# Cosine attention and a hard-swish layer: the fourth query tiles of a pair's two heads on two column halves of TensorE

## The chip, the cores and the metric

The kernel runs on one core of a Trainium2 chip. The metric is the device time of one execution in microseconds; a kernel's figure is the median of several executions. Profiles and traces come from one profiled execution.

## The reference

Attention over 8 batches and 12 heads, sequence length 448, head dimension 64. Queries and keys are divided by their norms, scores are divided by tau and go through a softmax; the result, laid out as 3584 tokens of 768 features, goes through a feed-forward layer with a hard-swish.

```
q_n = q / (norm(q) + 1e-06);  k_n = k / (norm(k) + 1e-06)
attn = softmax(q_n @ k_n^T / tau)
x = (attn @ v) as [3584, 768]
h = x @ w_in                       # 768 -> 2048
out = (h * clip(h + 3, 0, 6) / 6) @ w_out   # 2048 -> 768
```

## The kernel before

**Tiling.** Two heads are worked on together as a pair; there are 48 pairs, six for each batch. The 448 tokens are cut into three tiles of 128 and a rest of 64. Scores are computed transposed: keys on the 128 partitions, queries along the free dimension. The keys of a pair fall into four groups (`GROUPS`, L364): in groups 0 to 2 each head has a 128-key tile of its own (A0 and B0, A1 and B1, A2 and B2), and group 3, "M", joins the last 64 keys of both heads in one 128-partition tile. `scores` (L367) makes a group's scores in PSUM: for groups 0 to 2 two matmuls on the two 64-row halves of the array, since the head dimension is 64; for group 3 one matmul with all 128 rows, against `km`, which holds both heads' keys block by block. `exps` (L400) writes the exponentials as bf16 to an `at` tile, [128 keys, 1 or 2 heads, 512 queries]; its columns 448 to 511 are padding that was set to 1 once (L680).

**Value products.** `values(i, g)` (L421) multiplies one group's exponentials with the values. `at` is the stationary operand, 128 queries at a time, so that the result has queries on partitions. The moving operand is `vx`: 64 value columns and a column of ones for each head, 65 columns, so that the sum of the softmax comes out beside the result. There are four query tiles j; the fourth holds 64 queries and 64 columns of padding. In groups 0 to 2 each head has four matmuls of 65 columns (eight in a group); in group M each query tile has one matmul of 130 columns, as both heads' values lie side by side with zeros where the other head's keys are. All 28 matmuls of a pair add up in one PSUM tile `PV`, [128, 2 banks, 512]; `pv_out(j)` (L414) gives the place of query tile j in it, [128, 2 heads, 65]: tiles 0 and 1 in the first bank, 2 and 3 in the second. The first product in each bank starts the accumulation for the whole bank.

**After the products.** `finish_values(i)` (L444) runs on VectorE: the reciprocal of the eight sums (L453), then one multiplication of all of `PV` with them into the bf16 tile `on` (L454). A transposing DMA on SP's queue (`back_crossbar`, L485, for one pair, `back_two`, L497, for two) brings `on` to `xT`, where tokens are along the free dimension. When a batch's six pairs are there, `mm1_unit` (L513) does a 128-wide slice of the first feed-forward matmul, with the hard-swish on ScalarE (L522) and VectorE (L528), and `mm2_unit` (L549) a slice of the second, with copies out (L560, L562) and stores (L570).

**Order.** The order of every engine's queue is written out by hand. Up to pair 17 a list of strings, `PLAN`, gives it; from pair 18 a loop (L699) does. An iteration i of the loop issues the scores of pair i, groups 0 to 2, with their exponentials; the value products of pair i - 1, groups 1 to 3; `finish_values(i - 1)`; the scores of pair i, group 3; then the transposing DMA, the feed-forward units that belong to this iteration, the preparation of later pairs (squares, norms, transposes, loads); and last the value products of pair i, group 0.

```
for g in range(1, 4):
    if ("VA", i - 1, g) not in issued:
        do("VA", i - 1, g)
do("FI", i - 1)
do("SC", i, 3)
do("EX", i, 3)
```

So TensorE sees, in each iteration: six score matmuls on 64-row halves, 20 value products, one score matmul with all rows, a few dozen feed-forward matmuls, and 8 value products. After the last pair its remaining products follow directly, then the feed-forward units that are left.

Of the kernel before, what the change touches and what calls it, by code (L numbers as in the profile page):

```python
# [11 lines left out]
ALU = mybir.AluOpType  # L12
# [3 lines left out]


FIRST = 18
ORDER = "111111111111111111111111111111222222"

PLAN = [
# [40 lines left out]
def kernel(  # L62
# [10 lines left out]
    nc = tc.nc  # L73
    B, H, S, D = q.shape
# [8 lines left out]
    SM = 384  # L83
# [60 lines left out]
    def needs(*what):  # L144
        for w in what:
            assert w in issued or any(x < 0 for x in w[1:] if isinstance(x, int)), w
# [217 lines left out]
    GROUPS = [("A0", "B0"), ("A1", "B1"), ("A2", "B2"), ("M",)]  # L364
# [49 lines left out]
    def pv_out(j):  # L414
        return PV[:, j // 2, 0:260].rearrange("p (j h e) -> p j h e", j=2, h=2)[:, j % 2, :, :]


    def q_cols(b, j):
        return slice(128 * j, 128 * j + 128)

    def values(i, g):  # L421
        needs(("VC", i), ("FI", i - 1), *([("VA", i, g - 1)] if g else []))
        at = at_of.pop((i, g))
        vt = vx[i % NVX]
        last = g == len(GROUPS) - 1
        for n, name in enumerate(GROUPS[g]):
            for j in range(4):
                if name == "M":
                    o, mv = pv_out(j), vt[:, 3:5, :]
                else:  # L430
                    h = "AB".index(name[0])
                    o, mv = pv_out(j)[:, h, :], vt[:, 5 * h + int(name[1]), :]
                nc.tensor.matmul(  # L433
                    o,
                    at[:, n, q_cols(i // HP, j)],
                    mv,
                    start=(name == "A0" and j % 2 == 0),
                    stop=last,
                    skip_group_check=True,
                )  # L440

    twin_on = {}

    def finish_values(i):  # L444
        needs(*(("VA", i, g) for g in range(4)))
        if i % 2 == 0:
            needs(("BK", i - 4), ("BK", i - 3))
            twin_on[i // 2] = sb.tile([128, 2, 4, 2, D], BF16, name="on", tag="on", bufs=2)
        rc = sb.tile([128, 2, 4], FP32, name="rc", tag="rc", bufs=2)
        on = twin_on[i // 2][:, i % 2, :, :, :]  # L450
        on_of[i] = on
        pv4 = PV[:, :, 0:260].rearrange("p b (n e) -> p b n e", e=D + 1)
        nc.vector.reciprocal(out=rc[:, :, :], in_=pv4[:, :, :, D])  # L453
        nc.vector.tensor_tensor(  # L454
            out=on[:, :, :, :].rearrange("p (b j) h d -> p b (j h) d", b=2),
            in0=pv4[:, :, :, 0:D],
            in1=rc[:, :, :].to_broadcast([128, 2, 4, D]),
            op=ALU.mult,
        )

    def back(i, bank=None):
        z, key = bank_of(bank, 1)
        if bank is not None:
            z = z[:, :].bitcast(BF16)
        z_of[-1 - i] = z, key
        on = on_of.pop(i)
        for j in range(4):
            c, e = (slice(128 * j, 128 * j + 128), slice(0, 128)) if j < 3 else (slice(SM, S), slice(0, SR))
            if bank is not None:
                c = slice(128 * j, 128 * j + 128)  # L470
                nc.tensor.transpose(z[:, c], on[:, j, :, :], ident[:, :])
                continue
            nc.tensor.matmul(z[:, c], on[:, j, :, :], ident[:, e], start=True, stop=True)
# [164 lines left out]
    def whole_units(n):  # L638
# [7 lines left out]
        "LQ": load_qk, "LV": load_v, "W": next_weights, "SQ": square, "RE": reduce, "NO": norms,  # L646
        "NM": normalise, "VC": vcast, "TR": transposes, "XD": crossbar, "XB": back_crossbar, "XP": back_two, "CQ": copy_q, "CK": copy_k, "CS": copy_k3, "SC": scores,
        "EX": exps, "VA": values, "FI": finish_values, "BK": back, "CX": copy_x, "U": unit, "UA": lambda: finish_units("a"), "UV": lambda: finish_units("v"),
        "UU": whole_units, "D": busy, "DP": busy_pv, "OPEN": open_ring,
    }  # L650

    def do(op, *args):
        OPS[op](*args)
        key = (op,) + tuple(a for a in args if isinstance(a, int))
        if op not in ("RE", "NM", "LQ"):
            issued.add(key[:3] if op == "SC" else key)
# [31 lines left out]
    by_kind = {"1": [u for u in stream if u[0] is mm1_unit], "2": [u for u in stream if u[0] is mm2_unit]}  # L688
    first = [by_kind[x].pop(0) for x in ORDER]
    stream = first + [u for u in stream if u not in first]  # L690
# [5 lines left out]

    if FIRST + 6 < NP:
        do("LQ", FIRST + 6)
    for i in range(FIRST, NP):  # L699
        n_u = len(units[i])  # L700
# [84 lines left out]
```

## Time and profile before

| | |
|---|---|
| median of 8 runs | 424.08 us (422.91 to 426.73) |
| the profiled execution | 424.15 us, of which the trace's span is 422.4 us |
| value products (L433) | 1152 of 65 columns, 192 of 130 columns |
| their weight loads | 1344 of 128 columns, 98 ns each, overlapping the matmuls |
| feed-forward matmuls (L513) | 768 of 448 columns |
| feed-forward matmuls (L549) | 880 of 384 columns, 32 of 192 |
| `on` (L454) | 48 of 691 ns |

The duration of a matmul in the trace is modelled[...]: a 65-column product is shown with 194 ns, but the next one starts about 30 ns later. What a matmul costs on a full queue is therefore read from the distance between starts, not from its duration. `128*128` or `64*64` in a line is the part of the array (rows by columns) that the instruction uses.

### The profile page before, as it was taken

The numbers are of one execution on the slowest core, as the hardware profiler recorded it, in microseconds if no ns is written. First come the engines' busy times: TensorE is split into PE (matmuls) and PEld (weight loads), VectorE is DVE, ScalarE is ACT, GpSimd is POOL, SyncE is SP. The second block draws the span as 40 slices with busy tenths as digits, with TensorE's granted clock in tenths as the row PEclk, the third lists the DMA queues.
The fourth block names the chain that finished last, engine by engine and source line by source line (L and its number), as shares of the span: only waits on it lengthen the run. The fifth ranks groups of instructions, "written<-read, shape, count | busy, mean of one in ns | idle before, by whom it ended". The sixth has DMA issues, their size and how long they took to land.

```text
span 422.4 us, 9241 instructions
## 1 busy us (share of the span) xinstructions
PE 412.4 (98%) x3591; PEld 244.2 (58%) x3591; DVE 218.0 (52%) x420; ACT 271.3 (64%) x588; POOL 179.9 (43%) x187
## 2 busy tenths in 40 slices
PE   7999999999999999999999999999999999999996
PEld 5656465555656556555556555555655555655564
DVE  6778778756435544465445554555554343315410
ACT  4999888887648656757756775776765775105400
POOL 7697783363047256266365465364462200000000
PEclk9999999999999999999999999999999999999999
DMA  8999999997775867966974858757864431330033
GB/s 305 266 244 163 245 253 214 258 215 206 175 173 116 183 179 137 188 167 131 193 187 120 199 146 171 173 160 147 188 151 80 84 67 33 70 75 21 0 76 75
DMA packets 93740, 65.82 MB, mean 156 GB/s; under 512 B 58240, under 2 KB 92160, under 8 KB 93696
## 3 DMA queue, kind: packets, MB, share of 16 engines
q1 hardware_dynamic: 89904, 58.89, 60.9%
q0 software_dynamic: 3712, 6.29, 8.1%
q8 instruction: 28, 0.46, 0.5%
q14 instruction: 16, 0.13, 0.2%
q10 hardware_dynamic: 80, 0.05, 0.1%
HBM read 47.19 MB, written 11.01 MB: 138 GB/s over the span
## 4 chain that ended last, share of the span: by engine, by line
PE 90%; DMA 5%; DVE 1%; POOL 1%; issue 1%; ACT 1%; SPq 0%; POOLq 0%; ACTq 0%
PE M L549 23%; PE M L513 22%; PE PV L433 11%; PE Z L513 7%; PE Y L549 6%; PE M L394 6%; PE Y L513 5%; PE Z L549 5%; DMA raw<-in_k_dram 4%; PE Z L394 1%; PE PV L620 1%; DMA xT<-on 1%; PE Y L394 1%; PE SC L394 1%; DVE n L215 1%
## 5 line engine op out<-in xcount | busy, mean ns | idle before, releaser
L549 PEld LDWEIGHTS <-gT 128*128 128x128 bf16 x912 | 88.7, 98 | 58.4
L412 ACT ACTIVATE at<-M 128x448 bf16<-128x448 f32 x200 | 97.1, 566 | 31.1 <-PE M L394 28.7
L513 PEld LDWEIGHTS <-w_in_sb 128*128 128x128 bf16 x768 | 73.6, 98 | 66.1 <-issue 3.0
L513 PE MATMUL M<-xT,w_in_sb 128*128 128x448 bf16 x510 | 104.7, 353 | 0.1
L549 PE MATMUL M<-w_out_sb,gT 128*128 128x384 bf16 x592 | 100.8, 326 | 0.0
L246 POOL TENSOR_TENSOR nrm<-raw,r 128x896 bf16<-128x896 f32 (+1 forms) x46 | 75.3, 1639 | 33.4 <-ACT r L234 23.0
L528 DVE SCALAR_TENSOR_TENSOR gT<-u,M 128x448 bf16<-128x448 bf16 x85 | 52.4, 620 | 51.1 <-ACT u L522 49.7
L203 POOL TENSOR_TENSOR sq<-raw 128x896 f32<-128x896 f32 (+2 forms) x39 | 63.7, 1632 | 11.4 <-DMA raw<-in_q_dram 6.8
L433 PEld LDWEIGHTS <-at 128*128 128x128 bf16 x1344 | 53.7, 98 | 23.2 <-issue 15.9
L522 ACT ACTIVATE u<-M,bias 128x448 bf16<-128x448 f32 x85 | 54.9, 649 | 17.7 <-PE M L513 16.4
L433 PE MATMUL PV<-vx,at 128*128 128x65 bf16 (+1 forms) x1344 | 63.6, 198 | 0.0
L351 POOL COPY km<-tT 64x128 bf16<-64x128 bf16 x34 | 9.8, 289 | 107.4 <-DMA tT<-nrm 52.4
L215 DVE TENSOR_REDUCE n<-sq 128x14 f32<-128x896 f32 (+1 forms) x50 | 51.5, 1040 | 3.1 <-POOL sq L203 2.6
L560 ACT COPY o<-M 128x384 f32<-128x384 f32 x18 | 8.7, 481 | 41.2 <-PE M L549 39.3
L562 DVE COPY o<-M 128x384 f32<-128x384 f32 x19 | 10.6, 558 | 47.0 <-PE M L549 34.2
L454 DVE TENSOR_TENSOR on<-PV,rc 128x512 bf16<-128x512 f32 x48 | 33.2, 691 | 1.7
L394 PE MATMUL M<-tT,kz 64*128 64x448 bf16 (+1 forms) x178 | 33.4, 354 | 0.3 <-ACT at L412 0.3
L412 ACT ACTIVATE at<-Y 128x448 bf16<-128x448 f32 x47 | 26.6, 566 | 9.7 <-PE Z L394 9.7
L549 PE MATMUL Y<-w_out_sb,gT 128*128 128x384 bf16 (+1 forms) x192 | 31.9, 319 | 0.0
L513 PE MATMUL Z<-xT,w_in_sb 128*128 128x448 bf16 x144 | 31.2, 353 | 0.0
L412 ACT ACTIVATE at<-Z 128x448 bf16<-128x448 f32 x47 | 26.6, 566 | 7.1 <-PE M L394 4.1
L265 POOL CAST vx<-vr 128x512 bf16<-128x512 f32 x43 | 26.1, 612 | 5.7 <-DMA vr<-in_v_dram 5.1
(73 smaller groups left out, 329.7 us busy)
## 6 DMA issues: line engine op xcount, KB each, us to landing
vr<-in_v_dram SPq DMA_DIRECT2D x96, 128.0 KB, 4.2
raw<-in_q_dram SPq DMA_DIRECT2D x24, 448.0 KB, 4.5
raw<-in_k_dram SPq DMA_DIRECT2D x24, 448.0 KB, 4.5
out_dram<-o SPq DMA_DIRECT2D x110, 96.0 KB, 2.2
w_in_sb<-in_moe_w_in_dram POOLq DMA_DIRECT2D x4, 768.0 KB, 13.9
w_out_sb<-in_moe_w_out_dram POOLq DMA_DIRECT2D x4, 768.0 KB, 10.8
tT<-nrm SPq DMA_TRANSPOSE x34, 3.1
xT<-on SPq DMA_TRANSPOSE x29, 4.0
```

The costliest lines, as they stand in the source:

```text
L203: engines[e].tensor_tensor(out=o, in0=i, in1=i, op=ALU.mult)
L215: nc.vector.tensor_reduce(out=n2s[d % 2][:, j % 2, c], in_=sq[:, :, :, :].rearrange("p g c d -> p (g c) d")[:, c, :], axis=AX.X, op=ALU.add,)
L246: engines[e].tensor_tensor(out=nrm[:, :, g, :].rearrange("p c g d -> p g c d"), in0=raw_of[j][:, g, :, :], in1=rs[d % 2][3][:, j % 2, :] . ...
L265: (engines[e].copy if e == "a" else engines[e].tensor_copy)(out=o, in_=f)
L394: nc.tensor.matmul(o, ks, qt[rows], start=True, stop=True)
L412: nc.scalar.activation(out=o, in_=x, func=AF.Exp, scale=inv_tau)
L433: nc.tensor.matmul(o, at[:, n, q_cols(i // HP, j)], mv, start=(name == "A0" and j % 2 == 0), stop=last, skip_group_check=True,)
L454: nc.vector.tensor_tensor(out=on[:, :, :, :].rearrange("p (b j) h d -> p b (j h) d", b=2), in0=pv4[:, :, :, 0:D], in1=rc[:, :, :].to_broad ...
L513: nc.tensor.matmul(ps[:, 0:S], w_in_sb[:, cc, fc * 128 : (fc + 1) * 128], x[:, cc, 0:S], start=(cc == 0), stop=(cc == CC - 1),)
L522: nc.scalar.activation(out=u[:, :], in_=ps[:, 0:S], func=AF.Relu, bias=half_bias, scale=1.0 / 6.0)
L528: nc.vector.scalar_tensor_tensor(out=g[:, fc, c0 : c0 + S], in0=u[:, :], scalar=1.0, in1=ps[:, 0:S], op0=ALU.min, op1=ALU.mult,)
L549: nc.tensor.matmul(ps[:, 0:width], lhs, w_out_sb[:, fc, cols], start=(fc == 0), stop=(fc == FCN - 1),)
```

## The change

From pair 19 on (`TAILS`), the fourth query tile is left out of the products of each group. Its 64 queries are done behind the group M products of the same pair: for each of the four groups and each of the two heads one matmul with 64 columns of `at` (without the padding) as the stationary operand and 65 moving columns. Head 0's results go to partitions 0 to 63 of the fourth tile's place in `PV`, head 1's to partitions 64 to 127, so that the two heads' matmuls use the left and the right 64 columns of the array. For group M the 64 rows of the other head are cancelled by the zeros in `vx`, as before. Since head 1's queries of the fourth tile now lie on partitions 64 to 127, `finish_values` gets a third VectorE instruction, which multiplies that block with its reciprocals and writes it to partitions 0 to 63 of `on`, where the large multiplication had put something else.

```diff
+TAILS = 19
...
         last = g == len(GROUPS) - 1
+        tail = i >= TAILS
         for n, name in enumerate(GROUPS[g]):
-            for j in range(4):
+            for j in range(3 if tail else 4):
...
                     start=(name == "A0" and j % 2 == 0),
-                    stop=last,
+                    stop=last and not tail,
                     skip_group_check=True,
                 )
-
+        if not tail:
+            return
+        tail_of.append((g, at))
+        if not last:
+            return
+        for g, at in tail_of:
+            for h in range(2):
+                m = len(GROUPS[g]) == 1
+                nc.tensor.matmul(
+                    pv_out(3)[64 * h : 64 * h + 64, h, :],
+                    at[:, 0 if m else h, SM:S],
+                    vt[:, 3 + h if m else 5 * h + g, :],
+                    start=False,
+                    stop=m,
+                    skip_group_check=True,
+                )
+        tail_of.clear()
+
+    tail_of = []
...
             op=ALU.mult,
         )
+        if i >= TAILS:
+            nc.vector.tensor_tensor(
+                out=on[0:64, 3, 1, :],
+                in0=pv4[64:128, 1, 3, 0:D],
+                in1=rc[64:128, 1, 3:4].to_broadcast([64, D]),
+                op=ALU.mult,
+            )
```

## The prediction

> **What bounds the kernel now.** I read the page first: busy shares, then the slices with the granted clock.
>
> ```profile
> span 422.4 us, 9241 instructions
> PE 412.4 (98%) x3591; PEld 244.2 (58%) x3591; DVE 218.0 (52%) x420; ACT 271.3 (64%) x588; POOL 179.9 (43%) x187
> PE   7999999999999999999999999999999999999996
> PEclk9999999999999999999999999999999999999999
> ```
>
> TensorE is at 98%, VectorE at 52%, and the clock is whole. A busy PE can hide bubbles, because matmul ends are modelled, so I asked for the stretch that the change touches (pairs 19 to 47; their products run from 134 to 361 us) and then for the chain of waits inside one pair, number 35.
>
> ```profile
> core 0: us, PE busy (x) PEld busy (x) DVE busy (x) ACT busy (x) POOL busy (x), PEclk, DMA share, GB/s
> 161.00:361.00 200.00, 199.93 (x1735) 117.53 (x1734) 97.07 (x173) 131.33 (x295) 88.67 (x87) 1.00 0.64 142
> ```
>
> ```profile
> 261.33 2.60 PE Y L549 x16
> 263.94 0.24 PE PV L433 x8
> ...
> 264.85 0.08 PE Y L394
> 264.93 0.83 PE PV L433 x20
> 265.76 0.19 PE Z L394
> 265.95 0.19 PE M L513
> ```
>
> The chain never leaves PE in this pair. Over the 200 us one wait stands on it, 0.24 us at 176.7 us. So in this stretch a nanosecond more or less on TensorE's own queue is a nanosecond on the end.
>
> The same lines price a value product. Eight 65-column ones take 0.24 us, 0.030 each; over all 1056 neighbours in the instruction records the step from start to start is 30.9 ns in the mean (29 median), and 58 ns for the 130-column ones. In the x20 line 16 x 0.031 + 4 x 0.058 = 0.73 of 0.83 us; the other 0.10 us is something else. It stands where the score matmuls, which use 64 rows of the array (`64*128`), give way to full ones (`128*128`). I looked for such places where no semaphore can be the reason.
>
> ```profile
> 19.17 0.40 PE L433 MATMUL PV<-vx,at 128*128 128x130 bf16 x4
> 19.50 0.38 PE L391 MATMUL SC<-tT,kz 64*64 64x448 bf16 x2
> 19.81 0.28 PE L291 MATMUL Z<-ident,nrm 128*128 128x128 bf16 x2
> ```
>
> ```profile
> 63.95 0.39 PE L291 MATMUL Z<-ident,nrm 128*128 128x128 bf16 x4
> 64.26 0.36 PE L394 MATMUL M<-tT,kz 64*128 64x448 bf16 x2
> 64.56 0.55 PE L513 MATMUL M<-xT,w_in_sb 128*128 128x448 bf16 x2
> ```
>
> Read the starts (first column). The last of the four 130-column products starts at 19.17 + 0.40 - 0.22 (its modelled length) = 19.35 and streams for 0.058, to 19.41; the `64*64` pair starts at 19.50: 94 ns of nothing (151 - 57 in the records). Both its members start 3 ns apart and stream 448 columns in 0.187 to 0.189 us (six of L513 take 1.13 in the chain), to 19.69; the next full matmul starts at 19.81: 118 ns. At 64 us it is 98 in and 105 out. At 264.0 us, into the scores of the pair above, it is 96, and 39 neighbours of that kind in the trace have nearly the same step (median 125, mean 125.8 ns from start to start, 29 of it streaming). So each change of array shape costs about 95 ns in and 94 to 119 ns out, every time, and no other work lies beside it.
>
> **What the skill says.** "TensorEngine Tiling (Array Packing)", Key Properties: a change of tiling mode, as against a change of tile within a mode, drains TensorE. The gaps above agree, and in size they repeat. Its Restrictions add that column tiling turns fast weight load off. The trace has no `128*64` matmul; the nearest loads, 64 columns wide, are these:
>
> ```profile
> L433 PEld LDWEIGHTS <-at 128*128 128x128 bf16 x1344 | 53.7, 98 | 23.2 <-issue 15.9
> L391 PEld LDWEIGHTS <-kz 64*64 64x64 bf16 x12 | 0.6, 103 | 0.6 <-issue 0.2
> ```
>
> Half the columns, yet 103 against 98 ns, which fits. "TensorE: Matmul & The Clock Gate", Part 3, The mechanism, says that tiles of one mode start about 4 ns apart and run side by side; the trace shows 3 to 4 ns for row halves, nothing for column halves. The same page, LDWEIGHTS, prices a load by columns / 1.2 ns without the fast form: 53 ns for 64, used below as an estimate.
>
> **The change, part by part.** In the built program exactly TensorE's and VectorE's lists differ; ACT, POOL and SP have the same instructions in the same order with the same kinds of waits.
>
> Removed, for each of 29 pairs: query tile 3 of six 65-column groups and of the joint group, each with its load. 6 x 30.9 + 58 = 243 ns.
>
> Added on TensorE: eight loads and eight 65-column matmuls on `128*64` tiles, alternating between column 0 and column 64, between the joint group's third product and the pair's last score matmul (L394 on km, full shape). Both neighbours are full shape, so the block costs two changes of shape of its own; neither falls together with the change that the scores already pay, which lies 20 products earlier.
>
> - In: 94 ns (the `64*64` case). Out: 118 ns. The 3 ns of the second half, and 10 ns on the step behind (the second full matmul after a change starts 39 ns after the first at 264.9 us instead of 29). Together 225 ns. From the other side, by the row-halves' cheapest figures, 96 + 94 = 190.
> - Streaming: if halves run side by side and the loads go ahead behind the running matmul, four steps of 30.9 = 124 ns. If the halves go one by one, or the two loads of a step do, eight such steps, 247 ns. If a 53 ns load also stands in front of each step, 4 x (53 + 29) = 328.
>
> I take 225 + 124 = 349. The `64*64` gaps favour the two loads of a step going in parallel: its way out is 14 ns longer than the row halves' (302 against 288 ns from the last matmul's start to the next load), about the stream of 32 more columns, counted once and not twice. Net 349 - 243 = +106 ns a pair, x 29 = +3.1 us.
>
> Added on VectorE: one 64x64 multiply out of PSUM behind each pair's large one, waiting for it on VectorE itself (L454, 0.69 us). Nearest row:
>
> ```profile
> L313 DVE COPY kz<-Y 64x64 bf16<-64x64 bf16 x8 | 1.5, 187 | 0.5 <-PE Y L291 0.4
> ```
>
> With some 30 ns for the wait (the reciprocal, 208 ns, is followed 241 ns after its start) 0.22 us, 29 times, 6.4 us of VectorE work. Queued behind it are the products of hardswish (gT), which are not ready then (idle 1.49 us before the next one), and the transfer of `on` to xT, which SP issues later anyway:
>
> ```profile
> 266.04 0.69 DVE L454 TENSOR_TENSOR on<-PV,rc 128x512 bf16<-128x512 f32 x1
> ...
> 269.11 1.24 SPq L485 DMA_TRANSPOSE xT<-on  x1
> ```
>
> `on` is done at 266.73, SP comes to the transfer at 269.11 behind four V loads: 2.4 us of cover. For pair 47 the transfer does follow at once (362.37), but its reader, the first product with that batch's xT, is at 379.07, 12 us after landing. PV's next writer starts some 4 us later. I cost it at nothing; without cover it would be at most 0.2 us in each of five batches, 1 us. The `at` and V buffers stay read a little longer, to the end of the same pair; their next writers come a whole pair later, and no wait is added for them. The last score matmul, and its exponential, come 0.1 us later; ACT is at 66% in this stretch (131.33 of 200).
>
> Sum: +3.1 us on the profiled execution, 424.15 us with a span of 422.4 and 1.75 around it; that is 0.07 above the median of 424.08. From the median: **427.1 us**, +0.7%.
>
> **Rivals.**
>
> - A, the forecast: two drains, halves side by side, loads hidden. +60 to +150 ns a pair, 425.8 to 428.5. For: every change of shape in the trace drains, and row halves do run together. 52%.
> - B: same drains, but no concurrency: halves or loads serialise at 247 ns. +229 a pair, +6.6 us, 430.7. For: no fast load, and four successive matmuls now add into the same PSUM words one step apart, where before at least four lay between. Against: the `64*64` loads. 27%.
> - C: the loads stand bare, 328 ns: +310 a pair, 433.1. 7%. The deep weight queue, seen everywhere (each load is recorded 1 to 2 ns behind the matmul before it), speaks against.
> - D, the other side: changing only the number of column tiles, with all 128 rows kept, doesn't drain. Then 124 + 10 - 243 = -109 ns a pair, -3.2 us, 420.9. It decides as soon as both changes together cost under about 119 ns. For: no `128*64` change is in the trace. Against: `64*64` after full, and `64*128` after `64*64`, drain alike (118 ns at 30.7 us). 9%.
> - E: one of the two changes is free: -243 + 124 + 95 to 118, some -15 ns, 423.7. 5%.
>
> That the change would not do what it says I set aside: the program has 116 matmuls on each of the two column tiles.
>
> **From these to the numbers.** This kernel's measurement tells about 0.5%, 2.1 us or 73 ns a pair, from no change. Faster by more: nearly all of D, 0.08. Within: E, the rest of D and the low end of A (under +73 ns), 0.15. Slower: the rest of A, B and C, 0.77. The range leaves out C, D and most of E: 424.9 to 431.3. A alone would have 425.8 to 428.5.
>
> **What would show it.** In the profile after, a group of `128*64` matmuls, 232 in all, starting in twos 3 to 4 ns apart, four steps of about 31 ns (A) or eight (B); some 95 ns empty ahead of them and 105 to 118 behind. The x20 piece becomes x15. PE stays at 98% and the chain on it; VectorE gains about 6 us and nobody waits for it. I am wrong if the gaps around the block are under 60 ns each (D), if the steps are over 50 ns (B, C), or if PE now idles for DMA, ACT or VectorE.

## The result, and the profile after

| | before | after |
|---|---|---|
| median | 424.0 us (32 runs) | 428.45 us (11 runs) |
| profiled execution | 424.15 us | 428.47 us |
| its span | 422.4 us | 426.7 us |

The ratio is 1.0104, 95% interval 1.0082 to 1.0125: the change costs about 4.4 us (3.5 to 5.3), 1.0%. The forecast was 3.1 us, so the sign and the main mechanism came out, and one term of the sum was off. The page after:

```profile
span 426.7 us, 9328 instructions
PE 417.7 (98%) x3620; PEld 243.6 (57%) x3620; DVE 224.5 (53%) x449; ACT 271.3 (64%) x588; POOL 179.9 (42%) x187
```

TensorE is still the bound. It is busy 5.3 us more, VectorE 6.5 us more, ScalarE and GpSimd as before. In the stretch from 161 to 361 us (busy time by engine, columns as in the prediction) PE has no gap at all, yet 1714 matmuls fit in where 1735 did, although a pair now has one more:

```profile
161.00:361.00 200.00, 200.00 (x1714) 113.97 (x1713) 101.95 (x196) 130.66 (x293) 88.76 (x87) 1.00 0.66 141
```

The new instructions, by form (busy us, mean ns of one, idle us before it):

```profile
L451 PE MATMUL PV<-vx,at 128*64 128x65 bf16 x232 | 9.2, 201 | 0.0
L451 PEld LDWEIGHTS <-at 128*64 128x64 bf16 x232 | 6.0, 110 | 3.1
L481 DVE TENSOR_TENSOR on<-PV,rc 64x64 bf16<-64x64 f32 x29 | 6.5, 226 | 1.0
```

There are 232 = 29 x 8 of them. The 64-column load is shown with 110 ns against 98 for a full one. Pair 35's value products on TensorE's timeline, with the scores of the next pair between them, before (start us, duration us) and then after:

```profile
264.11 0.36 PE L394 MATMUL Z<-tT,kz 64*128 64x448 bf16 x1
264.11 0.73 PE L394 MATMUL M<-tT,kz 64*128 64x448 bf16 x4
264.58 0.35 PE L394 MATMUL Y<-tT,kz 64*128 64x448 bf16 x1
264.86 0.90 PE L433 MATMUL PV<-vx,at 128*128 128x65 bf16 x20
265.60 0.35 PE L394 MATMUL Z<-tT,km 128*128 128x448 bf16 x1
```

```profile
266.04 0.36 PE L395 MATMUL Z<-tT,kz 64*128 64x448 bf16 x1
266.05 0.73 PE L395 MATMUL M<-tT,kz 64*128 64x448 bf16 x4
266.58 0.35 PE L395 MATMUL Y<-tT,kz 64*128 64x448 bf16 x1
266.86 0.72 PE L435 MATMUL PV<-vx,at 128*128 128x65 bf16 x15
267.50 0.32 PE L451 MATMUL PV<-vx,at 128*64 128x65 bf16 x8
267.75 0.36 PE L395 MATMUL Z<-tT,km 128*128 128x448 bf16 x1
```

Two places differ. From the first value product behind the scores to the last score matmul (km) it was 0.74 us and is 0.89: the 15 products are followed by the block on the column halves. And the six score matmuls, from the first to the sixth (Z to Y), took 0.47 us and take 0.54, though nothing in them was changed.

The instruction records give the block in nanoseconds, and its length is the same within 3 ns in all 29 pairs. From start to start: 151 from the last full product to the first half product (58 of it streaming, 93 empty), then steps of 3, 49, 3, 33, 3, 29, 4, then 126 to the next full matmul (29 streaming, 97 empty), and the step behind that is 11 longer than usual (200 for 189). Summed: 93 + 124 + 29 + 97 + 11 = 354 ns.

The second place is the sixth score matmul. The scores start in twos on the two row halves, so that the sixth starts 3 to 4 ns behind the fifth if nothing holds it. Its distance from the fifth (its step, below), over 28 pairs:

| | step of the sixth score matmul | mean |
|---|---|---|
| before | 3 or 86 ns | 51 ns |
| after | 63 or 146 ns | 110 ns |

What it waits for is seen with VectorE beside it, before and after:

```profile
263.77 0.41 PE L433 MATMUL PV<-vx,at 128*128 128x65 bf16 x8
263.97 0.56 DVE L562 COPY o<-Y 128x384 f32<-128x384 f32 x1 [3.33 <-PE Y L549]
...
264.58 0.35 PE L394 MATMUL Y<-tT,kz 64*128 64x448 bf16 x1
```

```profile
265.76 0.35 PE L435 MATMUL PV<-vx,at 128*128 128x65 bf16 x6
265.96 0.56 DVE L589 COPY o<-Y 128x384 f32<-128x384 f32 x1 [3.33 <-PE Y L576]
...
266.58 0.35 PE L395 MATMUL Y<-tT,kz 64*128 64x448 bf16 x1
```

PSUM banks are handed out in a ring of six (`ring`, L629 of the kernel before), so the sixth score always gets the bank of the last feed-forward unit. Here that is Y, and the unit's result is copied out of Y until 264.53 (266.52). In all 28 pairs of both kernels that copy ends 51 to 55 ns before the sixth score starts, and the semaphore that the score waits for is the copy's. The copy hangs on the end of the feed-forward unit, not on the products: from the first product (263.77, 265.76) to the sixth score it is 0.81 us before and 0.82 after, although there are eight products in one case and six in the other. The two values of the step are the two engines that copy: 86 and 146 where VectorE copies in 558 ns, 3 and 63 where ScalarE does in about 480. So two of the seven products removed from each pair stand ahead of a wait that ends at its own time. TensorE reaches the scores 60 ns earlier and waits 60 ns longer.

Set iteration against iteration (start of the first score to the next one's), the change costs 166 to 176 ns in 26 of 27 iterations: 354 for the block, less 243 removed, plus 60 not given back, is 171. In the one left out, with 90 ns, a wait for xT of 0.24 us before shrank to 0.16. The trace's start up to pair 20 took 134.05 us before and 133.32 after; over the traces of this study it goes from 133.1 to 136.6, so differences of spans are less sure than those of iterations.

### The profile page after: what moved, and what is told of

The parts are those of the page before. It is cut to its first block, busy times and chain, and to the rows that moved or that the text cites. A ratio compares the mean times of both kernels' runs of the same rounds, so it can differ in the third digit from the quotient of the medians.

```text
span 426.7 us, 9328 instructions
## 1 busy us (share of the span) xinstructions
PE 417.7 (98%) x3620; PEld 243.6 (57%) x3620; DVE 224.5 (53%) x449; ACT 271.3 (64%) x588; POOL 179.9 (42%) x187
## 4 chain that ended last, share of the span: by engine, by line
PE 94%; ACT 2%; DMA 1%; DVE 1%; POOL 0%; issue 0%; SPq 0%; ACTq 0%; POOLq 0%
PE M L540 23%; PE M L576 23%; PE PV L435 10%; PE Y L576 7%; PE M L395 7%; PE Z L540 6%; PE Y L540 5%; PE Z L576 5%; PE Z L395 2%; PE PV L451 2%; ACT at L413 2%; PE PV L647 1%; PE Y L395 1%; DMA raw<-in_q_dram 1%; PE SC L395 1%; PE Z L292 1%
## 5 line engine op out<-in xcount | busy, mean ns | idle before, releaser
L435 PEld LDWEIGHTS <-at 128*128 128x128 bf16 x1141 | 46.7, 97 | 24.8 <-issue 17.6
L435 PE MATMUL PV<-vx,at 128*128 128x65 bf16 (+1 forms) x1141 | 56.6, 198 | 0.0
L395 PE MATMUL M<-tT,kz 64*128 64x448 bf16 (+1 forms) x178 | 34.5, 353 | 0.3 <-ACT at L413 0.3
L473 DVE RECIPROCAL rc<-PV 128x8 f32<-128x8 f32 x48 | 9.9, 207 | 37.3 <-PE PV L451 32.7
```

What stands on the lines that cost most here:

```text
L395: nc.tensor.matmul(o, ks, qt[rows], start=True, stop=True)
L435: nc.tensor.matmul(o, at[:, n, q_cols(i // HP, j)], mv, start=(name == "A0" and j % 2 == 0), stop=last and not tail, skip_group_check=True,)
```

## The experiments

Theory 1: the loss is the block's two changes of shape (with their edges), plus 60 ns a pair that the bank wait takes back. The rivals are with each run. All ratios are to runs of the kernel before made beside those of the experiment (medians 423.91 to 424.46 us), with their 95% intervals; they are made from the single runs and can differ a little from the ratio of the medians. Lengths of iterations are against the kernel before, without the first one and the one with the xT wait. In the expected texts early_tails is number 4, early_g1 number 6 and early_g1_late_v number 7.

**1. The tails late but full width.** The deferred products use 128 query columns and the whole array.

```diff
         for g, at in tail_of:
-            for h in range(2):
+            for n, name in enumerate(GROUPS[g]):
...
-                    pv_out(3)[64 * h : 64 * h + 64, h, :],
-                    at[:, 0 if m else h, SM:S],
...
+                    pv_out(3) if name == "M" else pv_out(3)[:, h, :],
+                    at[:, n, q_cols(i // HP, 3)],
...
```

> The fourth tile's products stay full width (128 query columns, 28 products a pair as before) but stand behind the pair's others, as in the change; no 128*64 tiles, no third VectorE multiplication. Theory 1 (the change pays about 355 ns a pair for its block, and 60 of the 243 ns that it removes are not given back, because the two products missing ahead of the scores only make the sixth score matmul wait longer for its PSUM bank): the sixth score matmul's step grows from 3 / 86 ns to about 63 / 146 ns, +1.7 us against before, about 425.7 us. Rival (the whole excess is the change of array shape; the longer wait is a by-product of it): no growth of that step, 424.0 us.

Measured: 425.15 us, 1.0027 (1.0007 to 1.0048). The sixth step is 62 to 65 or 144 to 148 ns, and the iterations are 52 to 64 ns longer than before, with the same 28 full products in each. The first and the sixth score of the iteration shown above, and the late products:

```profile
266.93 0.36 PE L395 MATMUL Z<-tT,kz 64*128 64x448 bf16 x1
267.46 0.35 PE L395 MATMUL Y<-tT,kz 64*128 64x448 bf16 x1
268.29 0.41 PE L451 MATMUL PV<-vx,at 128*128 128x65 bf16 x7
```

From the first to the sixth score it is 0.53 us, as with the change, and not 0.47. Theory 1's second term is there without any column half; the rival falls.

**2. Both heads on one column half.**

```diff
-                    pv_out(3)[64 * h : 64 * h + 64, h, :],
+                    pv_out(3)[0:64, h, :],
...
```

> The change with both heads' tails on column half 0, one after the other; the results land where they belong, so the third VectorE multiplication is gone. Theory (the halves do run side by side, a pair of matmuls costs one step of 29 to 33 ns): eight steps in place of four, +4 x 30 = 120 ns a pair, +3.5 us against the change, about 432. Rival (the starts 3 ns apart are only records, the array does them one by one): the same time as the change, 428.4, with the block's length unchanged at about 400 ns.

Measured: 433.02 us, 1.0204 (1.0172 to 1.0236). The steps become 53, 35, 30, 33, 29, 34, 29; the block is 122 ns longer (524 against 401 from full matmul to full matmul). So in the change the halves do run side by side, and two 64-column loads, one for each half, fit into a step of 29 to 33 ns.

**3. Without the third multiplication on VectorE** (the `if i >= TAILS` block of `finish_values` deleted).

> The change without the third VectorE multiplication: head 1's queries of the fourth tile are left out of the output. Theory (that work is covered): 428.4, within 0.4 us of the change, and the sixth score matmul still waits 63 / 146 ns. Rival (the 29 multiplications delay the copies out of PSUM and with them the banks): up to 1 us faster, 427.4, with a shorter wait.

Measured: 428.66 us, 1.0121 (1.0079 to 1.0164); from iteration 20 to 47 the trace takes 221.50 us against 221.58 with it. The same 63 and 146 ns. It costs nothing that shows.

**4. The tails behind group 0,** ahead of the scores.

```diff
-        if not tail:
+        if not tail or g:
             return
...
-        for g, at in tail_of:
+        for t, at in [(0, at)] + [(t, at_of[(i, t)]) for t in range(1, 4)]:
...
```

> All tails of a pair moved from behind its group M products to behind its group 0 products, straight ahead of the next pair's scores: full, column halves, row halves, full, so three changes of shape an iteration in place of four, and the work stands where the sixth score matmul had to wait. Theory 1: first score 186 ns later than before (246 for the block and its way in, less 60), the wait of 44 ns in the mean gone, 182 ns of products gone behind the scores: -40 ns a pair, about -1.2 us against before, 422.9. Rival (column halves cost whatever stands beside them; only the number of blocks counts): as the change, 428.4, or 1 us less.

Measured: 424.55 us, 0.9992 (0.9965 to 1.0018): level with before, not the 1.2 us of gain. One iteration (start, duration):

```profile
141.04 0.34 PE L435 MATMUL PV<-vx,at 128*128 128x65 bf16 x6
141.32 0.32 PE L448 MATMUL PV<-vx,at 128*64 128x65 bf16 x8
141.57 0.36 PE L395 MATMUL Y<-tT,kz 64*128 64x448 bf16 x1
141.57 0.36 PE L395 MATMUL Z<-tT,kz 64*128 64x448 bf16 x1
141.77 0.54 PE L395 MATMUL M<-tT,kz 64*128 64x448 bf16 x4
```

The block now runs straight into the scores, and no sixth matmul stands apart: its step is 3 or 4 ns everywhere. The iterations are +14 to +21 or -58 to -66 ns against before, 29 less in the mean, where 40 was expected. The +14 to +21 are the iterations in which the kernel before lost no time at the sixth score (a step of 3 ns): there the block with its way in costs 246 ns against the 243 removed, and the first feed-forward matmul starts 200 to 204 ns behind the last score instead of 189, released by an exponential. So with one change of shape less the block just pays for itself, and the gain comes from the filled wait alone.

In the profiled execution one longer wait takes that gain back; it was 0.24 us before (waits of PE, 170 to 180 us: us in total, times, longest):

```profile
PE M L535 <- DMA xT<-on: 1.0, 1, 1.0
```

TensorE comes to this feed-forward matmul 4.4 us after the transfer's issue before and in number 4, but the transfer took 5.4 us and not 4.6. In the nine traces with V's loads ahead of it in SP's queue it took 3.4 to 5.4, so the wait need not be the same in every execution.

**5. Two products back ahead of the scores.** Column halves as in the change; two of group 1's products move ahead.

```diff
+        if tail and g == 0:
+            work += [(1, at_of[(i, 1)], 0, j) for j in range(2)]
+        if tail and g == 1:
+            work = work[2:]
...
```

> The change as it is, but two products of group 1 (head A, query tiles 0 and 1) are taken ahead of the scores, so that eight stand there again as before the change. Nothing else differs; the blocks on the column halves stay. Theory (the sixth score matmul waits for a PSUM bank whose copy-out ends at a fixed time after the last feed-forward unit; 60 ns fewer of products ahead of it are 60 ns more of waiting): its step goes back from 63 / 146 to 3 / 86 ns, -60 ns a pair, -1.6 us against the change, about 426.8; what remains against before, some 2.9 us, is the blocks. Rival (the wait belongs to the column halves, or follows whatever stands ahead): no change, 428.4.

Measured: 426.75 us, 1.0072 (1.005 to 1.0095). The step is 2 to 4 or 81 to 84 ns again, and the iterations are 106 to 118 ns longer than before, 60 less than the change's. The same iteration, first and sixth score, 0.47 us apart as before the change, and the block:

```profile
264.51 0.36 PE L395 MATMUL Z<-tT,kz 64*128 64x448 bf16 x1
264.98 0.35 PE L395 MATMUL Y<-tT,kz 64*128 64x448 bf16 x1
265.84 0.32 PE L457 MATMUL PV<-vx,at 128*64 128x65 bf16 x8
```

This separates the two terms: 111 for the block, net of what it saves, and 60 for the wait.

**6. All of group 1 ahead, without column halves.**

```diff
         do("VA", i, 0)
-    do("VA", NP - 1, 1)
+        if i >= 19:
+            do("VA", i, 1)
```

> The kernel before, without any column halves, with all of group 1's eight products taken ahead of the next pair's scores from pair 19 on (16 ahead, 12 behind). Theory (the same bank wait costs the kernel before 3 or 86 ns a pair, 47 in the mean, and 247 ns more of products fill it): step 3 everywhere, -47 ns a pair, -1.3 us, about 422.7. Rival (early_tails was level with before only because its fourth tiles are cheaper there): 424.0, no gain from order alone.

Measured: 424.82 us, 1.0009 (0.9991 to 1.0028): no gain. The sixth step is 3 ns in every pair, as expected, but the wait moved. The records show 264 to 268 ns from the last score matmul to the first feed-forward matmul, which should be 189, in every pair. An exponential releases that matmul: it reads the bank that the unit is to write. The exponentials start with the scores, and these came later. My expectation had left that chain out.

**7. Group 1 ahead, and V's loads later in SP's queue.** Number 6, and:

```diff
+        if even and i > FIRST:
+            prepare(("LV", (i + 4) // 2))
...
-        if not even:
-            prepare(("LV", (i + 5) // 2))
```

> As early_g1, and the loads of V stand behind the transposing DMA of on in SP's queue in place of ahead of it. Theory (the one wait for xT at about 176 us, 0.24 us before and longer when TensorE gets there earlier, is SP's queue order): -0.3 to -0.6 us against early_g1, about 422.3, no wait over 0.11 us on TensorE behind 130 us. Rival: the transfer itself is late, no change.

Measured: 424.08 us, 1.0005 (0.9986 to 1.0024); iteration for iteration as number 6, also where the xT wait was. Number 6 had no wait for xT left in its trace, so the move of the loads had nothing to give here, and neither side of the expectation is decided.

**8. Early tails, and V's loads later:** number 4 with number 7's edit of the loads.

> The early tails with V's loads behind the transposing DMA. Theory: the 1.1 us wait for xT at 176 us goes, about 1 us less than early_tails; per pair it then stands 33 ns under before, all of it from the filled bank wait (47) less 14 that the block still costs. So about 423.2, and not under early_g1_late_v. Rival (fourth tiles on column halves gain by themselves with three changes of shape): under early_g1_late_v by 1 us or more.

Measured: 424.16 us, 0.9986 (0.9966 to 1.0005). The iteration with the xT wait, 898 ns longer than before in number 4, is 215 shorter. SP starts that transfer 0.03 us after `on` is complete (170.89 to 170.92) instead of 2.2 us (169.52 to 171.71), it takes 3.4 us, as in the other two traces with the loads behind it (3.2 and 3.3), and TensorE comes to it 6.5 us after its issue. The gain against before can't be told from none.

**9. Four products ahead, no column halves, V's loads later.** As number 5 with four in place of two, on the kernel before, and the edit of number 7.

> The kernel before, no column halves; from pair 19 on head A's four products of group 1 go ahead of the next pair's scores (12 ahead, 16 behind), and V's loads stand behind the transposing DMA of on. Theory (the sixth score matmul waits at most 86 ns for its bank, 124 ns fill it; early_g1 failed since only 12 products, 479 ns, were left between the scores and the next feed-forward unit, which then waited 77 ns for a bank that an exponential still reads; 16 products leave 602 ns): both waits gone, -47 ns a pair, and the 0.24 us at 176 us, so -1.5 us, about 422.5. Rival (the bank chain through ScalarE takes back whatever comes ahead of the scores): a wait of some 30 to 70 ns ahead of the first unit, no gain, 424.0.

Measured: 422.57 us, 0.996 (0.9937 to 0.9983), faster than both kernels. One pair:

```profile
143.18 0.36 PE L394 MATMUL Y<-tT,kz 64*128 64x448 bf16 x1
143.18 0.36 PE L394 MATMUL Z<-tT,kz 64*128 64x448 bf16 x1
143.37 0.54 PE L394 MATMUL M<-tT,kz 64*128 64x448 bf16 x4
143.85 0.77 PE L439 MATMUL PV<-vx,at 128*128 128x65 bf16 x16
144.45 0.35 PE L394 MATMUL Y<-tT,km 128*128 128x448 bf16 x1
144.64 0.92 PE L519 MATMUL Z<-xT,w_in_sb 128*128 128x448 bf16 x4
```

The six scores are three close twos, and the unit starts 0.19 us after the last score. The iterations are level with before where ScalarE copies and 80 to 85 ns shorter where VectorE does, 48 less in the mean; number 8, with the column halves, has 30. The order and the loads were changed together, so this run doesn't say what each gave to the time.

**10. The block cut in two.**

```diff
-        if not last:
+        if g % 2 == 0:
             return
         for g, at in tail_of:
```

> The change with its tail block cut in two: the tails of groups 0 and 1 directly behind group 1's products, those of groups 2 and M at the end. The same matmuls, two more changes of shape in each pair. Theory (each block costs 93 ns in, 97 out, 20 on its first step and 11 on the step behind): +221 ns a pair, x 29 = +6.4 us against the change, 434.8. Rival (the cost lies in the small matmuls themselves): no more than 1 us longer than the change.

Measured: 434.71 us, 1.0233 (1.0192 to 1.0274). The same matmuls, 218 to 231 ns more in each iteration than with the change:

```profile
135.82 0.36 PE L435 MATMUL PV<-vx,at 128*128 128x65 bf16 x6
136.10 0.25 PE L451 MATMUL PV<-vx,at 128*64 128x65 bf16 x4
136.29 0.53 PE L435 MATMUL PV<-vx,at 128*128 128x65 bf16 x9
136.75 0.25 PE L451 MATMUL PV<-vx,at 128*64 128x65 bf16 x4
136.94 0.36 PE L395 MATMUL Z<-tT,km 128*128 128x448 bf16 x1
```

A further block costs some 226 ns, although no matmul was added; the rival falls.

## Why the prediction was right, and where it was short

**The bound.** Right, but for one place in each pair, the sixth score matmul (below): TensorE's queue sets the end, and its lengthening is what was measured.

**Two changes of shape.** Right. Column halves with all 128 rows leave TensorE empty on both sides (93 and 97 ns), as row halves do; rivals D and E fall. Forecast 225 ns around the streaming; number 10 gives 226 for one block. That the sum is so near is in part luck: the way out is 97 and not 118 ns, 21 under, while the block's own four steps take 153 and not 127, 26 over. The first of them is 49 and not 31. In pair 35 the loads of the second two are recorded 26 and 27 ns behind the first two's matmuls, later ones 2 to 3; that the loads set this step was not tested.

**Halves side by side, loads hidden.** Right, by number 2 and the later steps of 29 to 33 ns; rivals B and C fall. The 53 ns for a 64-column load, which I had estimated from the Trainium skill, "TensorE: Matmul & The Clock Gate", LDWEIGHTS, do not stand in front of each step: the steps would then be 82. In number 2 every step of 29 to 36 ns behind the first has one load of 64 columns for the same half. Whether the load is shorter than the estimate or only overlapped, no run here tells. The block as a whole: 349 forecast, 354 measured.

**The products removed.** This is the step that failed. The prediction counted "6 x 30.9 + 58 = 243 ns" as given back in full, since "a nanosecond more or less on TensorE's own queue is a nanosecond on the end". That held for the five products behind the scores. The two of group 0 stand ahead of the sixth score matmul, which waits for its bank's copy-out; they gave back nothing, and 183 ns remain of the term. Numbers 1 and 5 show it from both sides. So +106 ns a pair became +171, over the +150 at which case A ended. The wait comes 28 times, since no scores follow pair 47's first products: 29 x 0.111 + 28 x 0.060 = 4.9 us by the iterations in place of 3.1. The medians say 4.4, with 4.9 inside the interval of 3.5 to 5.3.

The sign was there to see. The chain quoted in the prediction has a piece of 0.08 us for the sixth matmul, which runs beside the fifth if nothing holds it and then adds none. After the change that piece reads

```profile
266.40 0.38 PE M L395 x4
266.78 0.14 PE Y L395
```

The prediction counted the 0.08 as work. The list of TensorE's waits has no entry for it from 150 to 361 us, in either kernel: the modelled duration of the fifth score, 0.35 us, covers it. Where ScalarE copies there was no sign at all: the step was 3 ns, yet the bank came free just as TensorE got there, and each nanosecond taken out ahead became a nanosecond of waiting. The prediction's own sign of being wrong, TensorE held by ScalarE or VectorE, thus came true in part without an idle PE in the profile.

**VectorE, SP and the buffers at nothing.** Right: by number 3 the third multiplication (226 ns, as 0.22 was estimated) costs nothing that shows, and no wait for `xT` or the buffers is new. The transfer of `on` had the cover that was claimed: SP came to it some 2 us after `on` was complete.

## What to carry to other kernels

Using parts of the array pays only if it saves more streaming than the two changes of shape cost, here some 226 ns a block against 119 ns saved (243 removed less 124 added). Beside a place that changes shape anyway, such a block came out level here (246 ns against 243, number 4), and the order alone, without column halves, was at least as good (number 9). Work taken out ahead of a wait that ends at its own time gives nothing back: before you count an instruction's removal, find what the next waiting instruction on that queue waits for, and how much later than its release it starts. A wait can hide as a short piece of a chain, or be just met and not show at all: compare the step of each matmul with its streaming time, also below 0.1 us.

## What the runs showed of the hardware that was not expected

A block on column halves leaves 93 ns empty going in and 97 to 101 coming out, whether it holds four matmuls (number 10) or eight. From column halves straight to row halves (number 4) the way is 126 ns from the last start, 29 of it streaming: 97 ns empty, once and not twice. The first step on column halves takes 49 to 53 ns, the later ones 29 to 36, alike with one head (number 2) or two in a step. Four successive matmuls that add into the same PSUM words 29 to 36 ns apart, start to start, showed no stall beyond this.
